# Weights from float64 on one Trainium2 core: the conversion spread over ScalarE and VectorE, with nothing left on GpSimd

## The chip, the core and the metric

The kernel runs on one core of a Trainium2 chip. The metric is the device time of one execution in microseconds. Engines are called as the profile calls them: PE (TensorE, matmuls; PEld its weight loads), DVE (VectorE), ACT (ScalarE), POOL (GpSimd) and SP (SyncE, which here issues all DMA transfers).

## What is computed

Attention with a window of 32 and 32 global tokens (4 batches, 8 heads, 512 local tokens, head size 64), then two layers of the form x, h = x W_in, g = f(h), y = g W_out:

```python
def _moe_ref(x, w_in, w_out, alpha):
    h = x @ w_in
    g = np.maximum(h, 0.0) + alpha * np.minimum(h, 0.0)
    return (g @ w_out).astype(np.float32)

def _moe2_ref(x, w_in, w_out):
    h = x @ w_in
    relu6 = np.clip(h + 3.0, 0.0, 6.0)
    g = h * relu6 / 6.0
    return (g @ w_out).astype(np.float32)
...
    x = np.ascontiguousarray(attn_out.transpose(0, 2, 1, 3)).reshape(B * S, H * D)
    x = _moe_ref(x=x, **moe_kwargs)
    return _moe2_ref(x=x, **moe2_kwargs)
```

There are 2304 tokens, the model width is 512, the inner width 2048. The weights w_in and w_out of both layers come as float64; the kernel is given their 64-bit words.

## The kernel before

Every product of the layers is made of three passes in the type fp32r: each operand is split into its value rounded to fp32r and the rest, and high x high, low x high and high x low are summed. So each weight has to be turned from float64 into float32 and then split.

**The conversion.** The weights of a layer come in 16 chunks (128 columns of w_in and 128 rows of w_out), each in two halves: a half tile is 128 partitions x 512 elements of 8 bytes, 512 KB. For each half tile `load_raw` (L96) issues the transfer into one of three `raw` buffers, `to_float32` makes the float32 in one of two `z` buffers, and `split_w` writes the two parts into `wt`. On the words of a double, `high` and `low`, each of them every second 32-bit element, this goes as follows. ACT, L107: r, the three bits of `low` that a float32 still needs (as their complement), in the one `r` buffer. DVE, L110: z = `high`, read as a float32, times 2^-112, which moves the exponent to a float32's. DVE, L111: shift left by 4 and right by 1. DVE, L113: the sign bit from `high`. DVE, L115: the last bits by exclusive or with r. ACT, L121: a copy of z rounded to fp32r into the first part of `wt`. POOL, L122: z minus that copy into the second part. This subtraction is all that POOL does in the kernel, apart from setting four constants.

**The stages.** Tokens are treated in five blocks, 512, 512, 512, 256 and 384 wide. In layer 1 the first block runs while w1 is converted, two half tiles for each of the 16 chunks, and while attention goes on in small steps (`attention_steps`); the first block is itself split into two lanes of 256, the second four chunks behind (DELAY). For each chunk `h_tile` makes 12 matmuls a lane (L355), `act` the activation (ACT L365, DVE L367, ACT L373, DVE L374), and `y_tiles` the 12 matmuls of the second product two chunks later (L386). Blocks two to four need no conversion. During the last block of layer 1 one half tile of w2 is converted a step, and during the first block of layer 2 the rest; there `act` takes the lines ACT L370, DVE L371, ACT L373, DVE L374, and the second product is L389. Layer 2 goes over the blocks in the order 1, 2, 0, 4, 3; the rows between the layers pass through DRAM (`evacuate`, L395 and L397, and `x_from_dram`). The conversion of w1 is called stage 1 in what follows, that of w2 stage 2.

**What sets the order.** A scheduler fixes the order of the instructions on each engine's queue when the program is built; each queue then runs in order. Tiles come from pools with a fixed number of buffers (`raw` 3, `z` 2, `r` 1, `t` 3, `g` 3), and an instruction that writes a buffer waits until the last reader of what was there before is done. The `wt` pool has 16 chunks, so w2's chunks take the place of w1's as the last block of layer 1 releases them.

Of the kernel before, what the change touches and what calls it, by code (L numbers as in the profile page):

```python
# [9 lines left out]
F32 = mybir.dt.float32  # L10
# [3 lines left out]
AF = mybir.ActivationFunctionType  # L14
ALU = mybir.AluOpType
# [36 lines left out]
def fused_kernel(ctx, tc, qT, kE, vE, qgT, kN, vN, vgN, w1, alpha, w2, mask, ident, out):  # L52
    nc = tc.nc
    pool = lambda name, bufs=1, **kw: ctx.enter_context(tc.tile_pool(name=name, bufs=bufs, **kw))

    const = pool("const")
# [42 lines left out]
    def to_float32(raw):  # L99

        words = raw.bitcast(U32).rearrange("p (f two) -> p f two", two=2)
        low, high = words[:, :, 0], words[:, :, 1]
        r = work.tile([128, 512], U32, tag="r", name="r", bufs=RB)
        nc.scalar.activation(r, low, AF.Relu, bias=seven_sb, scale=-(2.0 ** -29))  # L107
        z = work.tile([128, 512], F32, tag="z", name="z", bufs=ZB)
        bits = z.bitcast(U32)
        nc.vector.tensor_scalar(out=z, in0=high.bitcast(F32), scalar1=2.0 ** -112, scalar2=None, op0=ALU.mult)  # L110
        nc.vector.tensor_scalar(out=bits, in0=bits, scalar1=4, scalar2=1, op0=ALU.logical_shift_left,  # L111
                                op1=ALU.logical_shift_right)
        nc.vector.scalar_tensor_tensor(out=bits, in0=high, scalar=0x80000000, in1=bits, op0=ALU.bitwise_and,  # L113
                                       op1=ALU.bitwise_or)
        nc.vector.scalar_tensor_tensor(out=bits, in0=bits, scalar=7, in1=r, op0=ALU.bitwise_xor,  # L115
                                       op1=ALU.bitwise_xor)
        return z

    def split_w(raw, wt, m):
        z = to_float32(raw)  # L120
        nc.scalar.copy(wt[:, m, 0, :], z)  # L121
        nc.gpsimd.tensor_tensor(out=wt[:, m, 1, :], in0=z, in1=wt[:, m, 0, :].bitcast(F32), op=ALU.subtract)  # L122

    class Weights:

# [8 lines left out]
        def convert(self, halves):  # L134
            for _ in range(halves):
                k = self.next
                if k == 2 * NJ:
                    return
                if k == 0:
                    for i in range(RAW):  # L140
                        self.fetch(i)
                if k % 2 == 0:
                    self.wt[k // 2] = wp.tile([128, 2, 2, 512], F32R, tag="w", name="wt", bufs=NJ)
                split_w(self.raw.pop(k), self.wt[k // 2], k % 2)
                self.fetch(k + RAW)
                self.next += 1
# [245 lines left out]
    def evacuate(y, c, n, tags=("t",)):  # L392
        r = work.tile([128, 512], F32, tag=tags[c % len(tags)], name="ev", bufs={"t": TB, "z": ZB}[tags[c % len(tags)]])
        if c % 2:
            nc.vector.tensor_copy(r[:, :n], y[:, :n])  # L395
        else:
            nc.scalar.copy(r[:, :n], y[:, :n])  # L397
        return r
# [1 line left out]

    half_sb = const.tile([128, 1], F32, name="half_sb")
    nc.vector.memset(half_sb, 0.5)
    seven_sb = const.tile([128, 1], F32, name="seven_sb")
    nc.vector.memset(seven_sb, 7.0)

    x2 = [dram.tile([128, NC, n], F32, name=f"x2_{i}") for i, n in enumerate(width)]

# [94 lines left out]
    for k, bi in enumerate(order):  # L502
# [21 lines left out]
        for piece in blocks[bi]:  # L524
            for i in range(1 if piece == "g" else 2):
                r = evacuate(y[c], c, 512, ("t", "z"))
# [62 lines left out]
```

## Time and profile before

| | us |
|---|---|
| median of 3 runs | 908.92 (908.21 to 909.07) |
| the profiled execution | 909.61 |
| its span in the profile | 907.8 |
| busy: PE | 875.4 (96%) |
| busy: DVE | 471.7 (52%) |
| busy: ACT | 367.8 (41%) |
| busy: POOL | 90.0 (10%) |

The span runs from the first to the last instruction; 1.8 us lie around it. Busy shares are averages over stretches with different limits, so a stage has to be read by itself. Matmuls are pipelined and their ends are modelled, so a PE that is shown busy is not always at its peak; how many matmuls it issues in a stretch tells more. "Idle before" is the time in which an engine did nothing just ahead of an instruction, and the name behind the arrow is what ended it.

### The profile page before, as it was taken

Reading aid. Unit: us, or ns where it says so; the run is one execution under the profiler, and the core shown is the slowest. Engines: PE = TensorE matmul, PEld = TensorE weight load, DVE = VectorE, ACT = ScalarE, POOL = GpSimd, SP = SyncE. Lnnn points to the kernel's source line nnn. Section 1 sums busy time; section 2 is a strip of 40 time slices with the busy share of each in tenths; the row PEclk is TensorE's granted clock in tenths of the full one; section 3 lists DMA queues with packets and bytes.
Section 4 is the critical chain, followed back from the end, with each engine's and each line's share of the span. In section 5 each row is a group of like instructions: output and inputs, shape, how many; then the busy total and the mean of one; then the engine's idle time right before and its main releaser. Section 6 shows DMA issues by size and latency. Waiting matters only on the chain.

```text
span 907.8 us, 16784 instructions
## 1 busy us (share of the span) xinstructions
PE 875.4 (96%) x6824; PEld 753.2 (83%) x6824; DVE 471.7 (52%) x1086; ACT 367.8 (41%) x848; POOL 90.0 (10%) x68
## 2 busy tenths in 40 slices
PE   7899899999999999999998879999999999999998
PEld 4679889888888888789998758888888888899897
DVE  4999998532334333344489999633223322332332
ACT  5775655532343332244344554432223322332332
POOL 0333341000000000000033323100000000000000
PEclk9899999999999999999999979999999999999999
DMA  8976566422222210453324454002000100000000
GB/s 269 315 250 204 184 185 199 140 64 68 81 81 88 79 48 1 163 191 114 117 98 137 138 202 134 1 1 82 0 1 24 47 0 1 33 15 1 25 11 25
DMA packets 33426, 86.57 MB, mean 95 GB/s; under 512 B 4292, under 2 KB 15812, under 8 KB 31940
## 3 DMA queue, kind: packets, MB, share of 16 engines
q1 hardware_dynamic: 33348, 85.48, 28.7%
q8 instruction: 54, 0.88, 0.4%
q14 instruction: 24, 0.20, 0.1%
HBM read 76.55 MB, written 8.91 MB: 94 GB/s over the span
## 4 chain that ended last, share of the span: by engine, by line
PE 76%; DVE 16%; issue 4%; DMA 1%; ACT 1%; SPq 0%; DVEq 0%; ACTq 0%
PE h_ps L355 34%; PE o_ps L389 21%; PE y_ps L386 15%; DVE z L111 4%; DVE z L113 3%; PE s_ps L185 2%; DVE z L115 2%; DVE z L110 2%; DVE t L367 2%; DVE g L374 2%; PE pt_ps L209 1%; PE o_ps L221 1%; DMA x<-ev 1%; PE go_ps L311 1%; DVE p L194 1%
## 5 line engine op out<-in xcount | busy, mean ns | idle before, releaser
L355 PE MATMUL h_ps<-xt,wt 128*128 128x512 f32 (+2 forms) x2112 | 411.9, 344 | 12.3 <-DVE t L371 6.3
L355 PEld LDWEIGHTS h_ps<-xt,wt 128*128 128x128 f32 x2112 | 346.0, 190 | 58.0 <-DVE t L371 6.7
L386 PE MATMUL y_ps<-g,wt 128*128 128x256 f32 (+2 forms) x1152 | 213.5, 335 | 5.0 <-ACT g L373 4.4
L389 PE MATMUL o_ps<-wt,g 128*128 128x512 f32 x816 | 198.5, 391 | 0.0
L386 PEld LDWEIGHTS y_ps<-g,wt 128*128 128x128 f32 x1152 | 176.8, 191 | 22.8 <-ACT g L373 5.4
L389 PEld LDWEIGHTS o_ps<-wt,g 128*128 128x128 f32 x816 | 152.3, 188 | 30.4
L122 POOL TENSOR_TENSOR wt<-z,wt 128x512 fp32r<-128x512 f32 x64 | 89.8, 1403 | 488.4 <-ACT wt L121 487.1
L374 DVE TENSOR_TENSOR g<-t,g 128x512 fp32r<-128x512 f32 (+2 forms) x164 | 98.6, 601 | 60.2 <-ACT g L373 59.7
L371 DVE SCALAR_TENSOR_TENSOR t<-t,h_ps 128x512 f32<-128x512 f32 (+2 forms) x80 | 48.6, 607 | 156.4 <-ACT t L370 156.1
L373 ACT CAST g<-t 128x512 fp32r<-128x512 f32 (+2 forms) x164 | 89.5, 546 | 92.4 <-DVE t L371 49.4
L367 DVE SCALAR_TENSOR_TENSOR t<-t,c_sb,h_ps 128x256 f32<-128x256 f32 (+2 forms) x96 | 55.6, 588 | 130.7 <-ACT t L365 130.6
L370 ACT ACTIVATE t<-h_ps,half_sb 128x512 f32<-128x512 f32 (+2 forms) x80 | 49.8, 624 | 155.4 <-PE h_ps L355 153.0
L365 ACT ACTIVATE t<-h_ps 128x512 f32<-128x512 f32 (+2 forms) x84 | 43.1, 513 | 138.3 <-PE h_ps L355 132.0
L121 ACT CAST wt<-z 128x512 fp32r<-128x512 f32 x64 | 39.6, 620 | 78.9 <-DVE z L115 76.6
L115 DVE SCALAR_TENSOR_TENSOR z<-z,r 128x512 uint32<-128x512 uint32 x64 | 57.2, 894 | 3.7 <-ACT r L107 1.9
L113 DVE SCALAR_TENSOR_TENSOR z<-raw,z 128x512 uint32<-128x512 uint32 x64 | 54.3, 849 | 1.2
L198 ACT ACTIVATE p<-p,st 128x128 f32<-128x128 f32 x128 | 49.7, 391 | 8.8 <-DVE st L194 8.7
L107 ACT ACTIVATE r<-raw,seven_sb 128x512 uint32<-128x512 uint32 x64 | 49.0, 766 | 3.4 <-DVE z L115 3.4
L111 DVE TENSOR_SCALAR z<-z 128x512 uint32<-128x512 uint32 x64 | 49.8, 778 | 0.6
L185 PE MATMUL s_ps<-k_t,qz 128*32 128x128 f32 x1024 | 42.6, 290 | 4.6 <-DMA k_t<-in_kE 4.3
L185 PEld LDWEIGHTS s_ps<-k_t,qz 128*32 128x32 f32 x1024 | 29.2, 115 | 15.2 <-issue 7.2
L194 DVE CUSTOM_DVE_ANT_0 p<-s_ps,mask_sb 128x128 f32<-128x128 f32 x128 | 29.6, 285 | 2.6 <-PE s_ps L185 2.5
(65 smaller groups left out, 359.1 us busy)
## 6 DMA issues: line engine op xcount, KB each, us to landing
raw<-in_w SPq DMA_DIRECT2D x64, 512.0 KB, 3.9
v_t<-in_vE SPq DMA_DIRECT2D x32, 512.0 KB, 4.6
k_t<-in_kE SPq DMA_DIRECT2D x32, 240.0 KB, 4.2
gk<-in_kN SPq DMA_DIRECT2D x4, 1088.0 KB, 5.4
out<-ev SPq DMA_DIRECT2D x17, 256.0 KB, 2.4
qz<-in_qT SPq DMA_DIRECT2D x64, 64.0 KB, 3.6
gv<-in_vN SPq DMA_DIRECT2D x4, 1024.0 KB, 6.9
x<-ev SPq DMA_DIRECT2D x12, 256.0 KB, 2.6
```

What stands on the lines that cost most here:

```text
L111: nc.vector.tensor_scalar(out=bits, in0=bits, scalar1=4, scalar2=1, op0=ALU.logical_shift_left, op1=ALU.logical_shift_right)
L113: nc.vector.scalar_tensor_tensor(out=bits, in0=high, scalar=0x80000000, in1=bits, op0=ALU.bitwise_and, op1=ALU.bitwise_or)
L115: nc.vector.scalar_tensor_tensor(out=bits, in0=bits, scalar=7, in1=r, op0=ALU.bitwise_xor, op1=ALU.bitwise_xor)
L122: nc.gpsimd.tensor_tensor(out=wt[:, m, 1, :], in0=z, in1=wt[:, m, 0, :].bitcast(F32), op=ALU.subtract)
L185: nc.tensor.matmul(s[W * g:W * g + W, 128 * n:128 * n + 128], lhsT=q[:, h, 128 * i + W * g:128 * i + W * g + W], rhs=k[:, o:o + 128], star ...
L355: nc.tensor.matmul(ps[:, a:b], lhsT=wts[j][:, 0, wl, 128 * c:128 * c + 128], rhs=xt[c][:, xl, a:b], start=k == 0, stop=k == 3 * NC - 1)
L367: nc.vector.scalar_tensor_tensor(out=t[:, c:d], in0=t[:, c:d], scalar=c1_sb[:, j:j + 1], in1=ps[:, c:d], op0=ALU.mult, op1=ALU.add)
L370: nc.scalar.activation(t[:, a:b], ps[:, a:b], AF.Relu, bias=half_sb, scale=1.0 / 6.0)
L373: nc.scalar.copy(g[:, 0, a:b], t[:, a:b])
L374: nc.vector.tensor_tensor(out=g[:, 1, a:b], in0=t[:, a:b], in1=g[:, 0, a:b].bitcast(F32), op=ALU.subtract)
L386: nc.tensor.matmul(y[c][:, a:b], lhsT=wts[j][:, 1, wl, 128 * c:128 * c + 128], rhs=g[:, gl, a:b], start=first, stop=last)
L389: nc.tensor.matmul(y[c], lhsT=g[:, gl, 128 * c:128 * c + 128], rhs=wts[j][:, 1, wl, :], start=first, stop=last)
```

## The change

r is now made by one ACTIVATE as the bits themselves and not as their complement (0.9 x and + 0.25, then rounding to a whole number). The multiplication by 2^-112 goes from DVE to ACT (L111 of the changed kernel). One DVE operation shifts z left by 3 and puts in r's bits (L112), a second the sign (L114). The subtraction of the parts goes from POOL to DVE (L121). In the changed file the lines that stay have other numbers: L107 became L108, L121 became L120, L365 became L364, L367 became L366, L371 became L370, L373 became L372, L374 became L373, L395 became L394.

```diff
         words = raw.bitcast(U32).rearrange("p (f two) -> p f two", two=2)
         low, high = words[:, :, 0], words[:, :, 1]
         r = work.tile([128, 512], U32, tag="r", name="r", bufs=RB)
-        nc.scalar.activation(r, low, AF.Relu, bias=seven_sb, scale=-(2.0 ** -29))
+        nc.scalar.activation(r, low, AF.Relu, bias=quarter_sb, scale=0.9 * 2.0 ** -29)
         z = work.tile([128, 512], F32, tag="z", name="z", bufs=ZB)
         bits = z.bitcast(U32)
-        nc.vector.tensor_scalar(out=z, in0=high.bitcast(F32), scalar1=2.0 ** -112, scalar2=None, op0=ALU.mult)
-        nc.vector.tensor_scalar(out=bits, in0=bits, scalar1=4, scalar2=1, op0=ALU.logical_shift_left,
-                                op1=ALU.logical_shift_right)
+        nc.scalar.activation(z, high.bitcast(F32), AF.Copy, scale=2.0 ** -112)
+        nc.vector.scalar_tensor_tensor(out=bits, in0=bits, scalar=3, in1=r, op0=ALU.logical_shift_left,
+                                       op1=ALU.bitwise_or)
         nc.vector.scalar_tensor_tensor(out=bits, in0=high, scalar=0x80000000, in1=bits, op0=ALU.bitwise_and,
                                        op1=ALU.bitwise_or)
-        nc.vector.scalar_tensor_tensor(out=bits, in0=bits, scalar=7, in1=r, op0=ALU.bitwise_xor,
-                                       op1=ALU.bitwise_xor)
         return z
 
     def split_w(raw, wt, m):
         z = to_float32(raw)
         nc.scalar.copy(wt[:, m, 0, :], z)
-        nc.gpsimd.tensor_tensor(out=wt[:, m, 1, :], in0=z, in1=wt[:, m, 0, :].bitcast(F32), op=ALU.subtract)
+        nc.vector.tensor_tensor(out=wt[:, m, 1, :], in0=z, in1=wt[:, m, 0, :].bitcast(F32), op=ALU.subtract)
...
-    seven_sb = const.tile([128, 1], F32, name="seven_sb")
-    nc.vector.memset(seven_sb, 7.0)
+    quarter_sb = const.tile([128, 1], F32, name="quarter_sb")
+    nc.vector.memset(quarter_sb, 0.25)
```

The scheduler makes a new order of it. DVE's queue in the last block of layer 1, from one activation of h to the next, before:

```order
L367 SCALAR_TENSOR_TENSOR t<-t,c_sb,h_ps 128x384
L110 TENSOR_SCALAR z<-raw 128x512
L115 SCALAR_TENSOR_TENSOR z<-z,r 128x512
L111 TENSOR_SCALAR z<-z 128x512
L374 TENSOR_TENSOR g<-t,g 128x384
L113 SCALAR_TENSOR_TENSOR z<-raw,z 128x512
L115 SCALAR_TENSOR_TENSOR z<-z,r 128x512
L110 TENSOR_SCALAR z<-raw 128x512
L367 SCALAR_TENSOR_TENSOR t<-t,c_sb,h_ps 128x384
```

and in the changed kernel:

```order
L366 SCALAR_TENSOR_TENSOR t<-t,c_sb,h_ps 128x384
L114 SCALAR_TENSOR_TENSOR z<-raw,z 128x512
L121 TENSOR_TENSOR wt<-z,wt 128x512
L373 TENSOR_TENSOR g<-t,g 128x384
L121 TENSOR_TENSOR wt<-z,wt 128x512
L112 SCALAR_TENSOR_TENSOR z<-z,r 128x512
L366 SCALAR_TENSOR_TENSOR t<-t,c_sb,h_ps 128x384
```

Between two activations six operations on the weights have become four, and all of them have two tiles as inputs.

ACT's queue at the same place, before:

```order
L365 ACTIVATE t<-h_ps 128x384
L373 CAST g<-t 128x384
L121 CAST wt<-z 128x512
L107 ACTIVATE r<-raw,seven_sb 128x512
L365 ACTIVATE t<-h_ps 128x384
L121 CAST wt<-z 128x512
L107 ACTIVATE r<-raw,seven_sb 128x512
L373 CAST g<-t 128x384
```

and in the changed kernel:

```order
L364 ACTIVATE t<-h_ps 128x384
L120 CAST wt<-z 128x512
L108 ACTIVATE r<-raw,quarter_sb 128x512
L372 CAST g<-t 128x384
L120 CAST wt<-z 128x512
L111 ACTIVATE z<-raw 128x512
L364 ACTIVATE t<-h_ps 128x384
L111 ACTIVATE z<-raw 128x512
L108 ACTIVATE r<-raw,quarter_sb 128x512
L372 CAST g<-t 128x384
```

The multiplication L111, which waits for the raw tile and for a free z, stands between the activations of h and their copies.

## Rows read from the trace of the kernel before

**Rows 1.** Busy time (and instructions) by stretch: PE, PEld, DVE, ACT, POOL; granted clock, DMA share, GB/s

```profile
20.00:60.00 40.00, 33.26 (x484) 26.27 (x484) 38.77 (x112) 27.97 (x83) 14.04 (x10) 0.91 0.93 299
60.00:150.00 90.00, 85.02 (x967) 79.50 (x967) 88.27 (x203) 55.22 (x127) 30.73 (x23) 1.00 0.62 196
150.00:455.00 305.00, 304.35 (x3024) 259.39 (x3025) 119.56 (x383) 115.61 (x326) 0.00 (x0) 1.00 0.29 97
455.00:582.00 127.00, 115.01 (x558) 102.66 (x557) 117.99 (x172) 64.56 (x113) 45.00 (x32) 0.95 0.39 127
```

**Rows 2.** Chain of waits by line: first 20 to 150 us, then 455 to 582 us

```profile
by line: DVE z L111 14.5%; issue 13.8%; DVE z L113 11.3%; DVE z L115 11.2%; DVE z L110 8.2%; DVE t L367 5.9%; PE h_ps L355 5.9%; PE y_ps L386 5.8%; DVE g L374 5.6%; DVE p L194 4.7%; DVE st L200 2.3%; DVE xt L327 1.9%; ACT r L107 1.8%; DVE x
by line: PE o_ps L389 17.4%; PE h_ps L355 17.2%; issue 15.5%; DVE z L111 11.5%; DVE z L113 8.2%; DVE z L110 6.0%; DVE t L367 5.4%; DVE g L374 5.0%; DVE z L115 4.0%; DMA x<-ev 3.7%; DVE xt L327 2.5%; ACT wt L121 0.8%; ACT r L107 0.6%; DVE t 
```

**Rows 3.** Groups by shape, whole run: busy us, mean ns | idle before, releaser

```profile
L122 POOL TENSOR_TENSOR wt<-z,wt 128x512 fp32r<-128x512 f32 x64 | 89.8, 1403 | 488.4 <-ACT wt L121 487.1 <-PE o_ps L389 1.3
L374 DVE TENSOR_TENSOR g<-t,g 128x512 fp32r<-128x512 f32 x92 | 63.9, 695 | 37.8 <-ACT g L373 37.5
L115 DVE SCALAR_TENSOR_TENSOR z<-z,r 128x512 uint32<-128x512 uint32 x64 | 57.2, 894 | 3.7 <-ACT r L107 1.9
L113 DVE SCALAR_TENSOR_TENSOR z<-raw,z 128x512 uint32<-128x512 uint32 x64 | 54.3, 849 | 1.2
L111 DVE TENSOR_SCALAR z<-z 128x512 uint32<-128x512 uint32 x64 | 49.8, 778 | 0.6
L107 ACT ACTIVATE r<-raw,seven_sb 128x512 uint32<-128x512 uint32 x64 | 49.0, 766 | 3.4 <-DVE z L115 3.4
L110 DVE TENSOR_SCALAR z<-raw 128x512 f32<-128x512 f32 x64 | 29.7, 464 | 0.0
```

**Rows 4.** Tile z: ns min/median/max of each line, first and last start us

```profile
L111 DVE TENSOR_SCALAR z<-z x64: 410/424/1560, 18.8 to 573.2; 128x512 uint32<-128x512 uint32 x64
L113 DVE SCALAR_TENSOR_TENSOR z<-raw,z x64: 655/692/1796, 19.7 to 574.7; 128x512 uint32<-128x512 uint32 x64
L122 POOL TENSOR_TENSOR wt<-z,wt x64: 1267/1336/1888, 22.2 to 577.3; 128x512 fp32r<-128x512 f32 x64
```

**Rows 5.** Timeline in stage 2: start us, us, engine, line [idle before <-releaser]

```profile
503.15 0.42 DVE L110 TENSOR_SCALAR z<-raw 128x512 f32<-128x512 f32 x1
...
503.50 1.30 POOL L122 TENSOR_TENSOR wt<-z,wt 128x512 fp32r<-128x512 f32 x1 [2.08 <-ACT wt L121]
504.01 1.07 DVE L111 TENSOR_SCALAR z<-z 128x512 uint32<-128x512 uint32 x1
...
507.31 0.62 ACT L121 CAST wt<-z 128x512 fp32r<-128x512 f32 x1 [2.28 <-DVE z L115]
...
508.01 1.82 POOL L122 TENSOR_TENSOR wt<-z,wt 128x512 fp32r<-128x512 f32 x1 [3.21 <-ACT wt L121]
...
510.77 0.42 DVE L110 TENSOR_SCALAR z<-raw 128x512 f32<-128x512 f32 x1
```

**Rows 6.** PE's matmuls by shape, 455 to 582 us (columns as in rows 3)

```profile
L386 PE MATMUL y_ps<-g,wt 128*128 128x384 f32 x183 | 36.4, 347 | 4.5 <-ACT g L373 4.4
L355 PE MATMUL h_ps<-xt,wt 128*128 128x512 f32 x132 | 34.9, 415 | 7.5 <-DVE t L371 6.3 <-DVE xt L327 1.1
L355 PE MATMUL h_ps<-xt,wt 128*128 128x384 f32 x146 | 27.4, 334 | 0.0
L389 PE MATMUL o_ps<-wt,g 128*128 128x512 f32 x97 | 23.7, 394 | 0.0
```

**Rows 7.** Chain of waits in order of time: start us, us; 256, 512 and 384 columns wide

```profile
396.43 2.76 PE y_ps L386 x23
...
557.64 2.72 PE h_ps L355 x12
...
804.16 2.10 PE h_ps L355 x12
```

**Rows 8.** PE's matmuls of the layers by shape, 20 to 150 us

```profile
L355 PE MATMUL h_ps<-xt,wt 128*128 128x256 f32 x348 | 48.9, 289 | 4.2 <-ACT wt L121 3.5 <-POOL wt L122 0.3 <-DVE xt L327 0.2
L386 PE MATMUL y_ps<-g,wt 128*128 128x256 f32 x302 | 41.3, 288 | 0.5 <-DVE g L374 0.4
```

## The prediction

> **What bounds the kernel now.** I read first the table of busy time by stretch, to see which engine is full where. Between 20 and 150 us VectorE (DVE) is busy 38.8 + 88.3 = 127 of 130 us, and between 455 and 582 us 118 of 127 us; in the 305 us between these, PE is busy all but 0.7 us and DVE only 120 us [rows 1]. GpSimd (POOL) works in the two stretches alone: they are the conversion of w1 (stage 1) and of w2 (stage 2), 32 half tiles each. Next comes the chain of waits in each of the two stretches: in stage 1 the four DVE lines of the conversion head it, with 14.5, 11.3, 11.2 and 8.2%; in stage 2 they still hold 29.7% beside PE's lines [rows 2]. So DVE sets the pace in stage 1 and in the first part of stage 2, and PE elsewhere.
>
> Then I asked what one conversion costs DVE. The four lines take 464, 778, 849 and 894 ns on average, 2.98 us for a half tile [rows 3]. Their spread tells more: L111 takes 410 ns at least, 424 as a median and 1560 at most; L113 655, 692 and 1796 [rows 4]. The timeline of stage 2 shows what the long ones have beside them: L111 at 504.01 took 1.07 us, begun while POOL's subtraction of 503.50 (1.30 us long) ran, and ended just after it [rows 5]. Undisturbed, the four would take 0.42 + 0.42 + 0.69 + 0.69 = 2.22 us. So about 0.76 us of each half tile is DVE held up while POOL reads and writes the same tiles, 49 us over 64 half tiles.
>
> Last, how much a lighter DVE could give back at all. In stage 2 PE issues 183 + 146 matmuls 384 columns wide and 132 + 97 of 512 [rows 6]. Where nothing is late, twelve of 384 take 2.10 us and twelve of 512 2.72 us [rows 7], 0.175 and 0.227 us each: 57.6 + 52.0 = 110 us of work in 127 us. PE loses 17 us there, and the same rows name two waits for it, 6.3 us for DVE's L371 and 4.4 us for ACT's L373 [rows 6]; L373 itself waits for DVE's result. In stage 1 the 348 + 302 matmuls of 256 columns are worth 78 us at 23 in 2.76 us [rows 7, 8]; with attention's small ones PE needs between those 78 us and the 118 it is shown busy [rows 1], whose ends are modelled.
>
> **The change part by part.** A half tile now takes on ACT: r (as before), z = high word times 2^-112 (new), the rounding copy (as before). On DVE: shift and last bits in one operation (L112), the sign (L114), the subtraction (L121). On POOL nothing.
>
> Removed from DVE: L110, L111, L113 and L115, 2.98 us. Added: three operations of two SBUF inputs each over 128x512. For all three the nearest rows are L113's median of 692 ns [rows 4] and the subtraction L374 in the same shape and output type, 695 ns [rows 3]; 3 x 0.69 = 2.07 us. Bounds for one: 0.655 (the shortest L113) and 0.894 (L115's present mean, if the hold-ups stayed). I take 0.69, since no operation is left on POOL that could hold it. DVE saves 0.91 us a half tile, 29 us in each stage: stage 1 from 127 to 98 us, stage 2 from 118 to 89.
>
> Added to ACT: one multiply over 128x512 that reads every second word. Bounds are its plain copy of that size, 0.62 us [rows 5], and L107, which reads the other words and a bias, 0.766 us [rows 3]. I take 0.67, between them, since it has L107's reading and no bias tile. 32 x 0.67 = 21 us: ACT goes from 28.0 + 55.2 = 83 to 104 us in stage 1 and from 65 to 86 in stage 2. Nothing hides this in stage 1 except that ACT now is idle there for 47 us; if ACT had no slack, it would cost the 21 us itself.
>
> The same multiplication takes DVE a mean of 464 ns [rows 3], so the move from DVE to ACT makes the operation itself 0.2 us dearer, 13 us of engine time over 64 half tiles. In the sum that counts only where ACT paces a stretch, which is the first rival below. The Trainium skill (ScalarE: Activation LUTs, Rules for kernel authors) says to multiply on VectorE and not on ScalarE; for the single operation these rows agree with it, and by that rule alone the move would be a loss of those 13 us.
>
> Waits: ACT's queue gets an instruction that waits for w's transfer and for a free z buffer; behind it stand the exponentials and the activations of h. Before, DVE took that wait. L107 already waited on the same transfer in the same queue, so only the z buffer is new. The r buffer (one of them) comes free after DVE's first operation and not its last, which helps. POOL's 1.34 us at the end of each half tile's path becomes 0.69 on DVE plus queueing. On SyncE's queue the loads of w still wait for both engines' last reading of the raw tile, now the second of three DVE operations instead of the third of four; the transfers of attention stand behind them, so earlier release is a small gain that I count at nothing: in 20 to 60 us the DMA engines are 93% busy [rows 1].
>
> The pair of z buffers limits too. In the timeline a half tile takes its buffer at 503.15 (L110), POOL releases it at 509.83, and the next L110 on it comes at 510.77 [rows 5]: 7.6 us for a ring of two, 3.8 us a half tile. After the change its own work is 0.67 + 0.69 + 0.69 + 0.62 + 0.69 = 3.36 us, with four handoffs between ACT and DVE. A handoff to DVE cost 0.94 us there (POOL's end to L110), one to an idle engine 0.1 (ACT's end at 507.93, POOL's start at 508.01). At 0.7 each the ring takes 6.2 us, 3.1 a half tile, 99 us a stage: no tighter than the engines.
>
> Sum. Stage 1: DVE 98, ACT 104, ring 99 and PE somewhere between 78 and 118, all in order and feeding each other, and the first 40 us with full DMA. None can be had without gaps; now DVE as sole pacer has 2% of them. I take 10% over the largest, 116 us: 14 less. Range: 104 (26 less) to 126 (4 less). Stage 2: DVE 89 and ACT 86 are well below PE's 110; I take 113: 14 less; range 110 (17 less) to 121 (6 less). Between and behind the stages nothing changes: W2's buffers and blocks are the same. The profiled execution took 909.6 us (907.8 of span and 1.8 around it), 0.7 over the median of the runs shown: 909.6 - 14 - 14 = 881.6, **882 us**.
>
> **Rivals.** *ACT, or the ring, paces stage 1.* For it: 104 us of ACT work in order, with exponentials that wait for DVE and activations that wait for PE between the conversions. (The Trainium skill's rule named above points the same way.) Against it: ACT is idle for 47 of the 130 us now. Then stage 1 gives at most 4 us, and stage 2 its 6 to 14: 890 to 900, say 896. *PE takes all.* Everything fits under PE, both stages come to their floors: 909.6 - 26 - 17 = 867. Against it: full DMA until 60 us. *The hold-ups are not POOL's.* Then the three operations keep the 0.76 us between them, DVE does 2.83 instead of 2.98, and the time is 909.6 - 5 = 905 or, with the wait for ACT, unchanged: 908. Against it: the median of L111 is at its minimum, and the long one in the timeline ends with POOL's instruction [rows 4, 5]. The Trainium skill (SBUF — State Buffer, Who interferes with whom) says that GpSimd and VectorE lock each other out of a shared pair of ports for a whole instruction; the trace agrees, with 1.07 us instead of 0.42 for L111 beside POOL. *Slower: the z ring.* If each of the four handoffs costs 1.3 us, because both queues are full where POOL's was empty, the ring takes 3.36 + 5.2 = 8.6 us, 4.3 a half tile; 32 of them are 137 us instead of the 122 that 3.8 make, 15 us more in stage 1, and stage 2 about as now: 925. It decides from a handoff of (7.6 - 3.36) / 4 = 1.06 us on, close to the 0.94 seen to DVE; against it, those to ACT should be shorter.
>
> **How the numbers follow.** Forecast 0.70, ACT or ring pacing stage 1 0.14, PE taking all 0.07, hold-ups not POOL's 0.03, slower by the ring 0.06. 0.2% (1.8 us) is what a measurement can tell from no change. The forecast's own bounds are 909.6 - 26 - 17 = 867 and 909.6 - 4 - 6 = 900; with the upper 2 us, where little of it lies, left out, and most of the rivals with ACT and with PE inside, the range 867 to 898 holds some 8 in 10. Faster takes the first three cases and half of the fourth: 0.92; the same 0.02; slower 0.06.
>
> **What would show it.** Right: L112, L114 and L121 at 0.69 us with no tail above 0.8; z on ACT at 0.62 to 0.77; DVE's share in the two stages well under 0.9; PE's 6.3 us for the line that is now L370 gone; the stretch from 150 to 455 shifted but as long. Wrong: ACT near full in stage 1, or long idle times of ACT and DVE waiting in turn for z; DVE operations that stay long; or a time above 900.

## The result, and the profile after

The changed kernel takes 882.77 us (median of 4 runs, 881.77 to 885.39); the kernel before, run beside it, 908.80 (908.21 to 909.07). The ratio is 0.9719 (95% interval 0.9697 to 0.974): 26 us less. 882 was forecast. The total came out; of the steps that led to it, some did not, as the runs below show.

The profiled execution took 885.39 us, with a span of 883.6. Its busy time by stretch, in the columns of [rows 1]:

```profile
20.00:60.00 40.00, 32.68 (x488) 26.37 (x488) 31.74 (x106) 32.95 (x92) 0.00 (x0) 0.91 0.93 292
60.00:150.00 90.00, 89.67 (x1068) 86.47 (x1069) 73.59 (x193) 73.03 (x170) 0.00 (x0) 0.98 0.66 215
150.00:455.00 305.00, 304.35 (x2958) 259.71 (x2958) 120.30 (x374) 116.25 (x317) 0.00 (x0) 1.00 0.28 94
455.00:582.00 127.00, 126.32 (x625) 112.85 (x624) 88.13 (x145) 81.79 (x143) 0.00 (x0) 1.00 0.38 124
450.00:540.00 90.00, 89.32 (x469) 83.05 (x468) 82.46 (x138) 75.66 (x135) 0.00 (x0) 1.00 0.55 179
```

The chain of waits by line, first 20 to 150 us, then 455 to 582 us, against [rows 2]:

```profile
by line: PE h_ps L354 31.8%; PE y_ps L385 28.6%; DMA raw<-in_w 21.6%; PE s_ps L184 7.7%; PE pt_ps L208 3.9%; PE o_ps L220 3.4%; DMA v_t<-in_vE 2.3%; ACT z L111 1.8%; ACT r L108 1.8%; ACT p L197 1.0%; issue 0.7%; ACT xt L325 0.5%; ACT wt L12
by line: PE h_ps L354 40.6%; PE o_ps L388 27.7%; PE y_ps L385 16.6%; DMA raw<-in_w 4.5%; DVE xt L326 1.7%; DMA x<-ev 1.5%; DVE z L112 1.3%; DVE wt L121 1.3%; issue 1.1%; DVE z L114 1.0%; DVE g L373 0.8%; ACT z L111 0.5%; DVE t L370 0.5%; DV
```

The conversion's DVE lines, which held 45 and 30%, are gone or at 1.3% and less; PE's lines lead, and in stage 1 the transfers of w1. In stage 1 DVE has room now: 105 of 130 us where it had 127. The 88 of 127 us in stage 2, where it had 118, say less: w2's conversion now ends at 539 us (the last subtraction begins at 538.5) and not at 579, and while it runs, from 450 to 540 us, DVE is busy 82.5 of 90 us, 92%, as full as before (101.2 of 110, below). PE issues 625 matmuls between 455 and 582 us instead of 558; the mix of shapes is not the same, since the changed kernel is further on. The tile z after, ns min/median/max of each line, answers to [rows 4]:

```profile
L111 ACT ACTIVATE z<-raw x64: 640/672/713, 19.6 to 535.6; 128x512 f32<-128x512 f32 x64
L112 DVE SCALAR_TENSOR_TENSOR z<-z,r x64: 660/690/695, 20.3 to 536.4; 128x512 uint32<-128x512 uint32 x64
L114 DVE SCALAR_TENSOR_TENSOR z<-raw,z x64: 681/687/696, 21.0 to 537.1; 128x512 uint32<-128x512 uint32 x64
L121 DVE TENSOR_TENSOR wt<-z,wt x64: 680/686/694, 22.6 to 538.5; 128x512 fp32r<-128x512 f32 x64
```

No operation has a tail any more. PE's matmuls by shape from 455 to 582 us (busy, mean ns, idle before), against [rows 6]:

```profile
L354 PE MATMUL h_ps<-xt,wt 128*128 128x512 f32 x180 | 43.5, 390 | 0.7 <-DVE t L370 0.7
L388 PE MATMUL o_ps<-wt,g 128*128 128x512 f32 x155 | 37.2, 389 | 0.0
L385 PE MATMUL y_ps<-g,wt 128*128 128x384 f32 x158 | 29.5, 334 | 0.0
L354 PE MATMUL h_ps<-xt,wt 128*128 128x384 f32 x132 | 24.7, 334 | 0.0
```

Of the waits of 6.3 us for DVE and 4.4 for ACT, 0.7 is left. Where the time came from is read at two points. The first 384-wide matmul opens the last block of layer 1, when stage 1 has long ended and stage 2 has not begun; timeline of PE there, before and then after (start, length in us):

```profile
443.65 0.34 PE L355 MATMUL h_ps<-xt,wt 128*128 128x384 f32 x1
```

```profile
436.95 0.34 PE L354 MATMUL h_ps<-xt,wt 128*128 128x384 f32 x1
```

And the tile o_ps (count, ns min/median/max, first to last start in us), before and after; its first matmul is the second product of layer 2's first chunk, while w2's last conversions still run:

```profile
L389 PE MATMUL o_ps<-wt,g x816: 387/389/628, 543.5 to 903.2; 128*128 128x512 f32 x164
```

```profile
L388 PE MATMUL o_ps<-wt,g x816: 387/389/398, 519.7 to 879.0; 128*128 128x512 f32 x164
```

From that matmul to the last it is 359.7 us before and 359.3 after: nothing changed behind it. Stage 1 gave 443.65 - 436.95 = 6.7 us; between the two points 543.5 - 443.65 = 99.9 us became 82.7, 17.1 less. Forecast were 14 and 14. (The profiled execution is 2.6 us above the median of its runs, so its own sum is 24 us less, not 26.) The stretch of 99.9 us is the measure of stage 2 from here on; "first o" is the first start of o_ps.

### The profile page after: what moved, and what is told of

Read it like the earlier page. It is cut to its first block, busy times and chain, and to the rows that moved or that the text cites. A ratio compares the mean times of both kernels' runs of the same rounds, so it can differ in the third digit from the quotient of the medians.

```text
span 883.6 us, 16649 instructions
## 1 busy us (share of the span) xinstructions
PE 864.9 (98%) x6824; PEld 750.2 (85%) x6824; DVE 413.7 (47%) x1022; ACT 402.2 (46%) x912; POOL 0.2 (0%) x4
## 4 chain that ended last, share of the span: by engine, by line
PE 91%; DMA 5%; DVE 1%; ACT 1%; SPq 1%; issue 0%; ACTq 0%; DVEq 0%
PE h_ps L354 41%; PE o_ps L388 21%; PE y_ps L385 21%; DMA raw<-in_w 4%; PE s_ps L184 3%; PE pt_ps L208 1%; PE o_ps L220 1%; PE go_ps L310 1%; PE xt_ps L339 1%; DMA x<-ev 0%; PE gpt_ps L297 0%; PE gs_ps L270 0%; ACT z L111 0%; DMA v_t<-in_vE 0%; DVE xt L326 0%
## 5 line engine op out<-in xcount | busy, mean ns | idle before, releaser
L385 PE MATMUL y_ps<-g,wt 128*128 128x256 f32 (+2 forms) x1152 | 210.0, 333 | 0.0
L370 DVE SCALAR_TENSOR_TENSOR t<-t,h_ps 128x512 f32<-128x512 f32 (+2 forms) x80 | 48.7, 608 | 167.3 <-ACT t L369 167.1
L373 DVE TENSOR_TENSOR g<-t,g 128x512 fp32r<-128x512 f32 (+2 forms) x164 | 98.1, 599 | 61.1 <-ACT g L372 60.5
L372 ACT CAST g<-t 128x512 fp32r<-128x512 f32 (+2 forms) x164 | 89.7, 547 | 75.5 <-DVE t L370 46.3
L366 DVE SCALAR_TENSOR_TENSOR t<-t,c_sb,h_ps 128x256 f32<-128x256 f32 (+2 forms) x96 | 55.6, 590 | 133.7 <-ACT t L364 133.6
L364 ACT ACTIVATE t<-h_ps 128x512 f32<-128x512 f32 (+2 forms) x84 | 43.1, 513 | 139.7 <-PE h_ps L354 133.7
L108 ACT ACTIVATE r<-raw,quarter_sb 128x512 uint32<-128x512 uint32 x64 | 49.2, 769 | 17.0 <-DMA raw<-in_w 13.8
L112 DVE SCALAR_TENSOR_TENSOR z<-z,r 128x512 uint32<-128x512 uint32 x64 | 44.1, 688 | 14.4 <-ACT z L111 7.7
L121 DVE TENSOR_TENSOR wt<-z,wt 128x512 fp32r<-128x512 f32 x64 | 43.9, 687 | 7.9 <-ACT wt L120 7.6
L184 PE MATMUL s_ps<-k_t,qz 128*32 128x128 f32 x1024 | 40.5, 285 | 7.0 <-DMA k_t<-in_kE 6.3
L111 ACT ACTIVATE z<-raw 128x512 f32<-128x512 f32 x64 | 42.9, 674 | 7.7 <-DMA raw<-in_w 6.7
L114 DVE SCALAR_TENSOR_TENSOR z<-raw,z 128x512 uint32<-128x512 uint32 x64 | 44.0, 688 | 0.5
L120 ACT CAST wt<-z 128x512 fp32r<-128x512 f32 x64 | 39.4, 617 | 4.9 <-DVE z L114 2.6
```

The lines of the kernel that those rows point to most:

```text
L108: nc.scalar.activation(r, low, AF.Relu, bias=quarter_sb, scale=0.9 * 2.0 ** -29)
L112: nc.vector.scalar_tensor_tensor(out=bits, in0=bits, scalar=3, in1=r, op0=ALU.logical_shift_left, op1=ALU.bitwise_or)
L184: nc.tensor.matmul(s[W * g:W * g + W, 128 * n:128 * n + 128], lhsT=q[:, h, 128 * i + W * g:128 * i + W * g + W], rhs=k[:, o:o + 128], star ...
L366: nc.vector.scalar_tensor_tensor(out=t[:, c:d], in0=t[:, c:d], scalar=c1_sb[:, j:j + 1], in1=ps[:, c:d], op0=ALU.mult, op1=ALU.add)
L370: nc.vector.scalar_tensor_tensor(out=t[:, a:b], in0=t[:, a:b], scalar=1.0, in1=ps[:, a:b], op0=ALU.min, op1=ALU.mult)
L372: nc.scalar.copy(g[:, 0, a:b], t[:, a:b])
```

## The experiments

Three theories were on the table. *DVE's sum* (the prediction's): DVE does less, so both stages get shorter. *POOL's hold-ups*: what counts is that no DVE operation stands still beside POOL any more. Later a third, *the crowded order*: hold-ups cost because the fixed order has no room for them. All ratios are to the kernel before on the same chip.

**The subtraction alone.** The kernel before with one word changed.

```diff
-        nc.gpsimd.tensor_tensor(out=wt[:, m, 1, :], in0=z, in1=wt[:, m, 0, :].bitcast(F32), op=ALU.subtract)
+        nc.vector.tensor_tensor(out=wt[:, m, 1, :], in0=z, in1=wt[:, m, 0, :].bitcast(F32), op=ALU.subtract)
```

> The kernel before, with its subtraction moved from POOL to DVE and nothing else changed. Theory (DVE was held up by POOL for 0.76 us a half tile): the long tails of L110, L111, L113 and L115 vanish (L111 near 0.42 us throughout), DVE's work a half tile is 0.42 + 0.42 + 3 x 0.69 = 2.91 instead of 2.98 us, so DVE stays the pacer and the time is 900 to 909 us. Rival (the long operations have another cause, and the number of operations on DVE counts): DVE gets 0.69 x 64 = 44 us more and the time goes to 930 to 950 us.

Measured: 886.26 us (884.68 to 888.31), ratio 0.9745 (0.9726 to 0.9764). Both expectations missed, and this is the most telling run. Tile z of this kernel:

```profile
L111 DVE TENSOR_SCALAR z<-z x64: 397/420/429, 18.7 to 559.0; 128x512 uint32<-128x512 uint32 x64
L113 DVE SCALAR_TENSOR_TENSOR z<-raw,z x64: 649/684/694, 19.4 to 559.9; 128x512 uint32<-128x512 uint32 x64
L122 DVE TENSOR_TENSOR wt<-z,wt x64: 673/684/693, 22.1 to 562.5; 128x512 fp32r<-128x512 f32 x64
```

The tails are gone with POOL's work, so they were POOL's. But DVE's sum is hardly less: 0.42 + 0.42 + 0.68 x 3 = 2.89 us a half tile, against the 2.98 of [rows 3]. Its stretch from 450 to 560 us, and below it that of the kernel before:

```profile
450.00:560.00 110.00, 110.00 (x561) 100.18 (x560) 104.10 (x203) 64.39 (x113) 0.00 (x0) 1.00 0.45 146
```

```profile
450.00:560.00 110.00, 98.01 (x489) 89.43 (x489) 101.24 (x151) 55.66 (x100) 38.45 (x27) 0.94 0.42 137
```

DVE is busier than before (104.1 of 110 us against 101.2), and PE loses nothing (561 matmuls against 489). A full DVE is not what held PE up. Of the 26 us this one edit gives some 23.

**The subtraction back on POOL, the rest of the change kept.** The edit is the one above reversed, on the changed kernel.

> The changed kernel, with the subtraction back on POOL. Theory: L112 and L114 are held up beside POOL again (means of 0.9 to 1.1 us instead of 0.69), DVE's work a half tile is about 2.0 us with the hold-ups against 2.07 without, and the time is within 5 us of the changed kernel's 883: 878 to 890 us. Rival (an empty POOL is what gives the gain): any work on POOL costs most of it, 895 to 908 us.

Measured: 898.01 us (894.47 to 902.18), ratio 0.9875 (0.9842 to 0.9907): the rival's range. The profiled execution was the slowest of the four, at 902.18. DVE does two operations a half tile, and they are long again; DVE's groups from 450 to 560 us (busy us, mean ns, idle before):

```profile
L114 DVE SCALAR_TENSOR_TENSOR z<-raw,z 128x512 uint32<-128x512 uint32 x30 | 31.7, 1056 | 0.4
L112 DVE SCALAR_TENSOR_TENSOR z<-z,r 128x512 uint32<-128x512 uint32 x30 | 28.3, 942 | 12.0 <-ACT z L111 11.7 <-ACT r L108 0.2
```

DVE is busy 89.1 of these 110 us, less than in the run above, and waits 11.7 us for ACT; yet PE issues 509 matmuls instead of 561. Less work on DVE with POOL beside it is worse than more work without.

**The multiplication back on DVE.** The changed kernel, with L111 as it was.

```diff
-        nc.scalar.activation(z, high.bitcast(F32), AF.Copy, scale=2.0 ** -112)
+        nc.vector.tensor_scalar(out=z, in0=high.bitcast(F32), scalar1=2.0 ** -112, scalar2=None, op0=ALU.mult)
```

> The changed kernel, with the multiplication by 2^-112 back on DVE (0.42 us there instead of 0.67 on ACT). Theory: DVE's work a half tile is 2.49 us; in stage 2 that makes about 100 us, still under PE's 110, and stage 1 is set by transfers at first and PE later, so the time is 882 to 890 us. Rival (taking work from DVE to ACT is what paid): DVE gets 27 us back and the time is 897 to 910 us.

Measured: 882.37 us (882.22 to 883.78), ratio 0.9705 (0.969 to 0.9719), the time of the changed kernel. DVE's multiply takes 421 ns (median), ACT's 672; the move to ACT neither gives nor costs time, though it takes 0.42 us a half tile off DVE.

**Idle work on POOL.** The changed kernel, with four small subtractions on POOL for each half tile; they read wt's first part and write a tile that nobody reads. Nobody waits for them, and the order on the other engines is the same row by row.

```diff
+        for i in range(4):
+            part = wt[:, m, 0, 128 * i:128 * i + 128].bitcast(F32)
+            nc.gpsimd.tensor_tensor(out=scratch, in0=part, in1=part, op=ALU.subtract)
```

> The changed kernel, with idle work added on POOL: after each half tile four subtractions of 128x128 that read the rounded copy and write a scratch tile that nobody reads. The order of the instructions on PE, DVE, ACT and SP is the changed kernel's, and none of them waits for POOL. Theory (POOL and DVE hold each other up, and the delays fall on the activations queued behind, also when DVE is not full): the three conversion operations get long tails and means of 0.8 us or more, and the time is 888 to 902 us though DVE still has spare time in stage 2. Rival (only the sum of DVE's work against PE's counts; DVE has some 39 us to spare in stage 2): tails, but 881 to 886 us.

Measured: 895.99 us (894.22 to 897.71), ratio 0.9857 (0.984 to 0.9873). 13 us of the gain are gone, by work that has no part in the computation. Tile z of this kernel:

```profile
L112 DVE SCALAR_TENSOR_TENSOR z<-z,r x64: 653/808/891, 20.5 to 546.7; 128x512 uint32<-128x512 uint32 x64
L121 DVE TENSOR_TENSOR wt<-z,wt x64: 672/882/897, 22.9 to 549.1; 128x512 fp32r<-128x512 f32 x64
```

The tile of POOL's idle work:

```profile
L124 POOL TENSOR_TENSOR scratch<-wt x256: 400/727/1551, 22.8 to 551.9; 128x128 f32<-128x128 f32 x128
```

PE's groups that wait, 450 to 560 us:

```profile
L388 PE MATMUL y_ps<-g,wt 128*128 128x384 f32 x171 | 33.2, 338 | 3.5 <-ACT g L375 2.2 <-DVE g L376 1.4
L357 PE MATMUL h_ps<-xt,wt 128*128 128x512 f32 x108 | 29.3, 422 | 3.8 <-DVE t L373 3.4 <-DVE xt L329 0.4
```

The waits are those of the kernel before: for the activations' DVE line and for ACT's copy behind it. In stage 1 the idle work costs nothing: the first 384-wide matmul comes at 436.3 us (436.9 without it). The loss lies in stage 2: 93.9 us between the two points against 82.7.

**One more operation on DVE, POOL empty.** The kernel of the first experiment, with the sign operation done twice.

```diff
         nc.vector.scalar_tensor_tensor(out=bits, in0=high, scalar=0x80000000, in1=bits, op0=ALU.bitwise_and,
                                        op1=ALU.bitwise_or)
+        nc.vector.scalar_tensor_tensor(out=bits, in0=high, scalar=0x80000000, in1=bits, op0=ALU.bitwise_and,
+                                       op1=ALU.bitwise_or)
```

> The kernel with the subtraction alone moved to DVE (886 us), with the sign operation done twice: one more 0.69 us operation on DVE a half tile, POOL still empty. Theory that DVE's sum sets the pace once it is over PE's: DVE gets about 20 us more in each stage, is over PE's 110 us in stage 2, and the time is 903 to 916 us. Rival (without hold-ups DVE's sum does not matter): 885 to 892 us.

Measured: 902.01 us (901.65 to 903.24), ratio 0.9922 (0.9905 to 0.9938), just below the theory's range. Its parts are opposite. Stage 1 is 17.5 us longer than in the first experiment (first 384-wide matmul at 454.8 us against 437.3): there DVE's sum does bind, once it is 3.58 us a half tile. Stage 2 is not longer by more than 1.9 us (83.8 against 81.9 us between the two points), although DVE has 22 us more to do over the 32 half tiles; the last conversion only ends at 604 us instead of 562. So in stage 2 more work on DVE costs next to nothing, and hold-ups on DVE cost 11 us (idle work on POOL) to 17 us (the kernel before) there.

**Why: the order.** What differs is what stands ahead of the activations in DVE's queue. Timeline of DVE in the kernel before, where PE's wait of 6.3 us falls, with PE's row at its end (start, length, engine, line):

```profile
523.55 0.55 DVE L374 TENSOR_TENSOR g<-t,g 128x384 fp32r<-128x384 f32 x1
...
526.11 1.36 DVE L115 SCALAR_TENSOR_TENSOR z<-z,r 128x512 uint32<-128x512 uint32 x1 [0.34 <-ACT r L107]
...
528.30 1.74 DVE L113 SCALAR_TENSOR_TENSOR z<-raw,z 128x512 uint32<-128x512 uint32 x1
...
531.94 1.77 DVE L113 SCALAR_TENSOR_TENSOR z<-raw,z 128x512 uint32<-128x512 uint32 x1
...
535.27 0.56 DVE L395 COPY ev<-y_ps 128x384 f32<-128x384 f32 x1 [0.43 <-DMA x<-ev]
535.75 1.04 DVE L111 TENSOR_SCALAR z<-z 128x512 uint32<-128x512 uint32 x1
536.82 0.69 DVE L113 SCALAR_TENSOR_TENSOR z<-raw,z 128x512 uint32<-128x512 uint32 x1
537.43 0.68 DVE L371 SCALAR_TENSOR_TENSOR t<-t,h_ps 128x512 f32<-128x512 f32 x1
...
538.16 5.49 PE L355 MATMUL h_ps<-xt,wt 128*128 128x512 f32 x12 [6.28 <-DVE t L371]
```

Between L374 and the first L371 stand 15 conversion operations, and four of them are long. PE waits for L371 behind them. They are not all of this wait: one L395 stands there too, which waits for a transfer, and the chain of waits goes through that transfer for most of the 6.3 us (start, length in us):

```profile
530.48 4.70 DMA x<-ev
```

DVE itself was idle only 0.43 us for it. And this wait lies at the passage from layer 1 to layer 2; most of the loss lies ahead of it, in the last block of layer 1. From its first matmul of h to its last L367 (L366 in the changed kernel) it is 521.5 - 443.65 = 77.8 us before and 502.7 - 436.95 = 65.7 after: 12.1 of the 17.1 us.

The count below is therefore of that block. There a step of PE takes 24 x 0.175 = 4.20 us [rows 7]. In that time DVE has to do the two operations of an activation (0.61 + 0.55 us) and the conversions that the order puts between two activations. Counted in the order from the first step of the block that has conversions (the queues shown with the change are one such piece), before it is 66 operations in 12 steps, 1.375 half tiles a step. At the undisturbed 2.22 us that is 1.375 x 2.22 + 1.16 = 4.21 us: by this sum the scheduler has filled PE's step to the brim. With the held-up 2.98 us it is 5.26. The sum is a little too large as a time on DVE, because neighbouring operations overlap in the profile: L113 of 536.82 ends at 537.51, and L371 starts at 537.43. Three more runs tested this.

**Paced.** In stage 2 each half tile's r waits for the activation of its step, through a bias that a small ACT instruction makes from g; FIRST is thinned to match. POOL keeps its work. The same edit was made to the kernel before, to the one with idle work on POOL, and to the changed kernel as a control.

```diff
-FIRST = (1, 2)
+FIRST = (1, 1, 2)
...
-        nc.scalar.activation(r, low, AF.Relu, bias=seven_sb, scale=-(2.0 ** -29))
+        nc.scalar.activation(r, low, AF.Relu, bias=state.get("pace", seven_sb), scale=-(2.0 ** -29))
...
+    def set_pace(g):
+        p = work.tile([128, 1], F32, tag="pace", name="pace", bufs=4)
+        nc.scalar.activation(p, g[:, 0, 0:1].bitcast(F32), AF.Relu, bias=seven_sb, scale=0.0)
+        state["pace"] = p
...
                 gs[s] = act(0, h_tile(xt, W1.wt, parts), parts)
+                if last:
+                    set_pace(gs[s])
...
                 gs[j] = act(1, h_tile(xt, W2.wt, parts), parts)
+                if k == 0:
+                    set_pace(gs[j])
```

The kernel before, paced:

> The kernel before, POOL's subtraction and all, but in stage 2 every half tile's r waits for the activation of the step it goes with, so that the fixed order holds one half tile between two activations in the last block of layer 1 (4 VectorE operations instead of 5.3 on average) and 1.3 in the first block of layer 2. Theory of the crowded order: before loses 18.5 us of PE's time there because the order was laid out for undisturbed durations (2.22 us of VectorE a half tile) and packs 1.35 half tiles into a step of PE, which with the held-up 2.98 us no longer fits (1.35 x 2.98 + 1.05 of activations = 5.1 us against PE's 4.2); at one a step it fits (4.0), so most of the loss goes: 893 to 901. Rival, the hold-ups hurt by where they fall, however many conversions stand there: 904 to 912.

Measured: 893.42 us (893.18 to 894.46), ratio 0.9825 (0.981 to 0.984). Over 16 us of the 26 come back with nothing taken from POOL or from DVE. Tile z and POOL's group over the whole run:

```profile
L113 DVE SCALAR_TENSOR_TENSOR z<-raw,z x64: 651/693/1796, 19.8 to 581.0; 128x512 uint32<-128x512 uint32 x64
```

```profile
L122 POOL TENSOR_TENSOR wt<-z,wt 128x512 fp32r<-128x512 f32 x64 | 87.7, 1370 | 498.8 <-ACT wt L121 498.8
```

The stretch from 450 to 560 us, and PE's one waiting group (450 to 600 us):

```profile
450.00:560.00 110.00, 108.45 (x562) 100.03 (x561) 93.66 (x152) 65.97 (x126) 33.66 (x25) 1.00 0.43 137
```

```profile
L355 PE MATMUL h_ps<-xt,wt 128*128 128x512 f32 x197 | 47.3, 390 | 1.5 <-DVE t L371 1.5
```

The long operations are still there, up to 1.8 us; PE's waits fell to 1.5 us, and its 562 matmuls are as many as with POOL empty. There are fewer long ones, though: from 450 to 560 us the four operations of a half tile take 2.66 us on average, where they took 3.11 before. So this run does not change the order alone. An estimate of what that does by itself: 2.66 us in the old order would still make 1.375 x 2.66 + 1.16 = 4.8 us a step.

The changed kernel with idle work on POOL, paced:

> The changed kernel with idle work on POOL (896.0 us), paced in the same way: one half tile a step in the last block of layer 1 instead of 1.5. Theory of the crowded order: 3 VectorE operations at 0.84 us and 1.25 us of stretched activations are 3.8 us a step and fit into PE's 4.2, so the 12 us go: 882 to 888. Rival: 893 to 898.

Measured: 882.99 us (882.35 to 884.23), ratio 0.971 (0.9694 to 0.9727): the 13 us are all back (here too the hold-ups fell, from 2.52 to 2.30 us a half tile). The control, with POOL empty:

> The changed kernel paced in the same way, nothing on POOL: the control. Its steps fit already (1.5 x 2.07 + 1.05 = 4.2 us), so both theories expect 881 to 886, the same as the changed kernel's 882.8 within 3 us, with the conversion of w2 ending later than 538 us. If it is slower by more, the pacing itself costs (a late chunk in the first block of layer 2), and the two others have to be read against it.

Measured: 884.22 us (882.88 to 884.57), ratio 0.9719 (0.9704 to 0.9733): no change, as both expected. The pacing helps only where there are hold-ups. Put together: the half tiles that each order puts into a step, DVE's time for a step with undisturbed durations and with the means of that run's groups from 450 to 560 us, and the time between the two points:

| kernel | half tiles a step | undisturbed, us | measured, us | first 384-wide h to first o, us |
|---|---|---|---|---|
| before | 1.375 | 4.21 | 5.44 | 99.9 |
| changed | 1.49 | 4.24 | 4.24 | 82.7 |
| changed, multiplication on DVE | 1.31 | 4.42 | 4.40 | 82.4 |
| before, subtraction on DVE | 1.09 | 4.31 | 4.31 | 81.9 |
| the same, one more operation | 0.88 | 4.33 | 4.33 | 83.8 |
| changed, idle work on POOL | 1.49 | 4.24 | 5.07 | 93.9 |
| before, paced | 0.94 | 3.25 | 3.86 | 84.5 |
| idle work, paced | 0.97 | 3.17 | 3.53 | 81.8 |
| changed, paced | 0.97 | 3.17 | 3.17 | 81.8 |

The first six rows are orders which the scheduler made freely (the sixth is that of the changed kernel); they fill the step to 4.2 to 4.4 us at undisturbed durations, whatever the operations are. Where the measured sum is 4.4 or less, the stretch takes 82 to 85 us; the two with over 5 us take 94 and 100. The run with the subtraction back on POOL does not fit this table: its step is 1.54 x 2.00 + 1.29 = 4.4 us (3.3 undisturbed), as with the multiplication on DVE, but its stretch is 97.1. So DVE's sum is not enough to tell what an order costs. There ACT, which makes z in order between the activations, waits 12.5 us for held-up DVE operations; that this is its cause was not tested.

**What limits stage 1.** First w1's transfers: only the first three half tiles of w1 are loaded, and the other 29 conversions read them again (left out are these 15 MB and w1's values).

```diff
-            if k < 2 * NJ:
+            if RAW <= k < 2 * NJ and self.src is w1:
+                self.raw[k] = kept[k % RAW]
+            elif k < 2 * NJ:
                 self.raw[k] = load_raw(self.src, k // 2, k % 2)
+                if self.src is w1:
+                    kept.append(self.raw[k])
```

> The changed kernel with only the first three half tiles of w1 loaded; the other 29 conversions read those again (this leaves out 15 MB of transfers, and the values of w1). Theory (what stage 1 still loses from 20 to 60 us is transfers at full rate, which the change couldn't give back): PE's loss in that stretch falls by half or more and the time is 866 to 877 us. Rival (conversion on ACT and DVE, or the two z buffers, set the pace there): 880 to 885 us, unchanged.

Measured: 881.03 us (879.96 to 881.17), ratio 0.9683 (0.9667 to 0.9699), the rival's case: under 2 us for all of w1's transfers, though the chain of the changed kernel gives them 21.6% of stage 1, 28 us. A share of the chain is what ended last, not what would be saved: without it something else ends a little earlier. DMA is full without them at first; stretches of this run:

```profile
20.00:30.00 10.00, 6.37 (x104) 4.49 (x95) 8.61 (x29) 9.50 (x23) 0.00 (x0) 0.72 0.97 297
30.00:40.00 10.00, 10.00 (x122) 8.10 (x121) 8.84 (x28) 10.00 (x31) 0.00 (x0) 0.77 0.27 85
40.00:50.00 10.00, 10.00 (x169) 8.07 (x168) 8.85 (x33) 9.00 (x26) 0.00 (x0) 1.00 0.50 165
```

Up to 30 us attention's own transfers fill DMA, and PE, 64% busy in the first of these stretches, is granted 0.72 and then 0.77 of its clock. Then the place of the first conversions among attention's steps, later, and earlier with the multiplication on either engine:

```diff
-CONVERT = (3, 5, 7, 9)
+CONVERT = (7, 8, 9, 10)
```

> The changed kernel with the first conversions of w1 asked for at attention steps 7 to 10 instead of 3, 5, 7 and 9, so that the first loads of w stand behind two more units of attention in SyncE's queue. Theory (what is left of stage 1's loss up to 30 us is attention's own transfers at full rate): the first matmul of h comes 1 to 4 us earlier and the time is 878 to 883 us. Rival (the conversions' start is as much on the path): 883 to 889 us.

> The run in which only the multiplication went back to VectorE (882.4 us, span 880.4), with the four attention steps that go along with w1's conversion put earlier: chunks 1, 2, 4, 6 instead of 3, 5, 7, 9. Putting them later (7 to 10) made the first h 2.5 us earlier but the time 10 us longer. Theory: what stage 1 loses at its start is attention's own work and transfers, and PE's products after it are paced by when attention's steps come, so an earlier place gives back 1 to 5 us: 877 to 881, first h later than 32.0 us, the last y of block 0 before 159.7 us, and everything behind shifted as a whole. Rival: the places 3, 5, 7, 9 are at the optimum, and the earlier steps crowd VectorE and the DMA engines while the first weights come: 883 to 890, the last y of block 0 after 162 us.

> The changed kernel with the same earlier places (1, 2, 4, 6). Theory: 878 to 882 us, with the last y of block 0 before 163.3 us. Rival: 884 to 892. If this one loses where the one with the multiplication on VectorE gains, ScalarE's queue (multiplication ahead of the exponentials) is what limits the start of stage 1.

Measured: later 892.96 us (891.22 to 894.51), ratio 0.9823 (0.9807 to 0.9839), worse than either expectation; earlier 886.90 (886.11 to 889.76) with the multiplication on DVE and 886.40 (885.79 to 886.93) on ACT, both in the range of their rival (883 to 890 and 884 to 892). The place in the kernel is the best of the three, and at the earlier place too it makes no difference which engine multiplies. No run that does all of the work beats the changed kernel by more than its own runs differ. One rival was not tested: from 60 to 150 us PE is shown busy 89.7 of 90 us in the changed kernel, so PE itself may set this part of stage 1.

## Why the prediction came out, and where it did not

**The tails are POOL's, and go with it: right, shown.** The three new DVE operations take 0.69 us as forecast, z on ACT 0.672 (0.67 forecast, between 0.62 and 0.77). The rival that they were not POOL's fell with the subtraction alone, and idle work on POOL brings them back.

**"DVE saves 0.91 us a half tile, 29 us in each stage": the step that failed.** The saving is there, but it is not what made the kernel faster. With the subtraction alone DVE saves 0.09 us a half tile, and the time falls by some 23 us; with the multiplication back on DVE the saving is smaller by 0.42, and nothing changes. The prediction read a DVE that is 93 to 98% busy as the pace [rows 1]. In stage 2 it is as full without POOL, and PE loses nothing; the forecast's sign that DVE's share would fall well under 0.9 came in stage 1 (0.81), but not while w2 is converted (0.92). What set the time in stage 2 was the hold-ups in an order that gave DVE 4.2 us of work for a step of 4.2, and got over 5: spreading the same conversions wider recovers 16 us, in part by shortening the hold-ups too.

**Stage 2: 14 forecast, 17.1 measured.** PE's floor was rightly put at 17 us below, from rows 6 and 7, and the kernel comes to it. The mis-sized term is the 3 us of gaps left on top: PE's waits there are 0.7 us.

**Stage 1: 14 forecast, 6.7 measured.** The term taken was "10% over the largest", 116 us, as if the engines' sums set it. They do not: with the subtraction alone DVE is busy 124.5 of 130 us, with the whole change 105.3, and the first 384-wide matmul comes at 437.3 and 436.9. DVE's sum binds only above that (the doubled sign). What holds the stage at this length stays open: not w1's transfers, not the multiplication's engine, and neither an earlier nor a later place of the first conversions shortens it. The 6.7 is itself rough: with the multiplication on DVE, 0.4 us faster in the median, the profiled run (882.22) has that matmul at 433.35 us. The forecast was 7 us too much here and 3 too little in stage 2, and the profiled run is 2.6 us above its median; that these nearly cancel, so that the total is met within 1 us, is luck.

**Rivals.** *ACT or the ring paces stage 1*: no; ACT is busy 106 of 130 us (104 forecast), and with the multiplication, 0.67 us a half tile, taken from ACT again the time is the same. *PE takes all*: in stage 2 it did; in stage 1 not as forecast, 6.7 us where 26 were put. *The z ring, slower*: no; between two half tiles a z buffer stays empty 1.2 us in stage 1 and 0.5 in stage 2 (mean, from the last reader's end to the next L111), and the ring takes 3.5 and 3.0 us a half tile, where 3.1 were put for both.

**The Trainium skill's rule on multiplying** (ScalarE: Activation LUTs, Rules for kernel authors) holds for the operation, 672 ns on ACT against 421 on DVE. As a forecast of 13 us lost it failed: ACT had the room, and 882.77 and 882.37 us are the same.

## What to carry to other kernels

Where queues are fixed in advance, an operation that runs longer than the scheduler assumed delays everything laid out behind it, and an engine that waits for that, even if its own engine is not the one that bounds the kernel. How much that costs depends on the order: in stage 2 some 17 us here, and 2 to 3 with the same work spread out. Before lightening a full engine, count what stands ahead of the instruction that the bound engine waits for, and compare the sum at measured durations with the step it has to fit in, as a first sign and not as a proof. If hold-ups can't be removed, spread the work that is not yet due: here that recovered most of their cost.

## What the runs showed of the hardware

Not every DVE operation is held up. Beside POOL's work, DVE operations that read one SBUF tile and one PSUM tile keep their time, those that read two SBUF tiles do not; ns min/median/max of activations from 455 to 560 us, with idle work on POOL (six of the nine L373 ran beside it, at 673 to 677 ns):

```profile
L376 DVE TENSOR_TENSOR g<-t,g x20: 545/750/889, 455.8 to 554.7; 128x384 fp32r<-128x384 f32 x12, 128x512 fp32r<-128x512 f32 x8
L373 DVE SCALAR_TENSOR_TENSOR t<-t,h_ps x9: 673/675/690, 524.2 to 558.8; 128x512 f32<-128x512 f32 x9
```

The Trainium skill (SBUF — State Buffer, Who interferes with whom) says that a VectorE instruction with two SBUF inputs contends with a GpSimd instruction that reads SBUF, and one with at most one does not, outside certain fast modes; these rows agree. L110 and L111 of the kernel before have one SBUF input and were held up too, to 1.42 and 1.56 us at most; no run here shows in which mode they ran. The hold-up goes both ways: POOL's small subtractions take 400 ns at least and 1551 at most, the 35 of them with less than 0.1 us of such DVE operations beside them 400 to 403, and its large one in the second experiment 1264 to 2640.

PE's idle time can cost twice. In the kernel before, stretches of 10 us:

```profile
530.00:540.00 10.00, 3.72 (x13) 2.72 (x12) 9.36 (x16) 5.58 (x10) 2.60 (x3) 0.70 0.71 229
540.00:550.00 10.00, 10.00 (x37) 8.00 (x36) 8.73 (x15) 4.87 (x8) 2.75 (x2) 0.79 0.34 92
```

In the stretch in which PE was busy 3.7 of 10 us, the granted clock was 0.70 (a mean between its levels of 1.2 and 2.4 GHz), and in the next one 0.79, where PE, busy throughout, issued 37 matmuls. The changed kernel has 1.00 in both, and 46 matmuls in each. Not every gap does this: from 510 to 520 us of the kernel before PE was busy 7.4 of 10 us at a granted clock of 1.00.
